# A planner that orders a fused attention and MLP kernel: new cost rules, weight checks tied to columns of h, and one leg less

## The chip, the cores and the metric

The kernel runs on one core of a Trainium2 chip. Its time is the device time of one execution in microseconds; the runs before are given by their median. The profile is of one further execution. Engines: PE (TensorE, matmuls), DVE (VectorE), ACT (ScalarE), POOL (GpSimd), SP (the queue that issues all DMAs).

## What is computed

Attention over 4 batches of 8 heads, 768 positions, head size 64, in which each query sees a window of 128 positions and the first 4 positions (sinks); then an MLP over the 3072 tokens with the square of a ReLU between its two products:

```python
scores = scale * np.matmul(q, k.transpose(0, 1, 3, 2))
keep = is_sink | in_window
scores = np.where(keep, scores, -1000000000.0)
a = np.exp(scores - max); a = a / (sum + 1e-09)
x = (a @ v) as 3072 x 512
h = np.maximum(x @ w_in, 0.0)          # 512 x 2048
out = (h * h @ w_out)                  # 2048 x 512
```

The weights arrive as 64-bit floats; the kernel reads them as pairs of 32-bit words.

## The kernel before

**Tiles.** The tokens are cut into 8 chunks of 384 (half a batch each). A chunk has 4 head pairs, so there are 32 pairs, numbered s = 0 to 31. The hidden layer is cut into 16 slices of 128; one slice of one chunk is called a column of h, and there are 8 x 16 = 128 of them.

**Attention of a pair** (`attention`, from L376): SP loads q (L402), two parts of k (L397) and v (L409). Scores are matmuls into a PSUM bank (L475 for the first 8 pairs, L481 after that, where DVE, POOL and ACT first split k and q into a high and a low part: L433, L438, L444, L449). DVE adds the mask and takes the minimum (L458), ACT exponentiates (L464), DVE makes reciprocals of the sums (L521, L522), POOL or ACT scale P (L529, L527). For the first 8 pairs P is turned by PE (L630); for the others by DVE in blocks (L660, L664), four DMAs to a DRAM tile `via` (L677) and one DMA back into `PT` (L690). The value product (L718, L722) gives 128 rows of x, which ACT and DVE split into xh (L734) and xl (L739). Two buffers of x exist (`xs`), chosen by the number of the chunk modulo 2.

**A column of h** (`products`, L754 on): the first product is 4 steps of 3 matmuls, 128x384 (L770), into one of two banks. ACT makes r, the ReLU (L783), and gh, its square (L787); DVE multiplies the bank by r (L792) and takes gh off it, giving the low part gl (L799). The second product is 3 steps, one to a block of 128 tokens, of 3 matmuls, 128x512 (L813), into three banks that collect over the columns of a leg. At a leg's end these are copied to `ob` (L854, DVE and ACT in turn) and stored.

**Legs.** The order in which chunks and slices are visited is a list of legs: chunk 0 slices 0 to 7, chunk 1 slices 0 to 7, chunk 0 slices 8 to 15, chunk 1 slices 8 to 15, then each later chunk whole. Where a leg ends at slice 8, its sums are stored to a DRAM tile `part` (L865) and reloaded later (L841) and added (L847).

**Weights** (`row_steps`): 32 rows of 512 KB, each loaded by SP (L283), put together from its words by three DVE operations (L295, L302, L309), copied to a high part by ACT (L315), and a low part is taken by DVE or POOL (L319).

**Checks** (`check_steps`): this way of splitting holds only for weights in a certain range, so each half row is loaded once more (64 loads of 256 KB, L331) into one of two buffers, and ACT runs two operations over it with a sum (L336, L343). At the end DVE and PE make a flag of all sums; if it is set, a second, general version runs (it does not here).

**The planner** (`Plan`) fixes each engine's order before anything runs. A step has one or more engines with a modelled cost, a rank, and cells that it reads and writes. `order` takes the steps one after the other: of the steps that may start first on an engine within 0.03 us, that with the lowest rank. A DMA is modelled with a landing time of its own, at most 8 in flight; a step whose kind is `"port"` does not start while POOL runs. A rank is the number of a column, or a number relative to it; ranks only decide between steps that are ready, so a step without inputs, as a check's load, is taken as soon as its buffer is free. Every engine then carries out its own list strictly in order and waits at each step for that step's inputs:

```python
add(
    ("SP", 0.4, 3.2), rank - 1,
    lambda: nc.sync.dma_start(out=half().rearrange("p w t -> p (w t)"), in_=words[n // 2, :, n % 2]),
    writes=[cell],
)
```

In this example 0.4 is the time on the queue, 3.2 the landing time, `rank - 1` when it is due, `cell` one of the two check buffers.

## Time and profile before

| | us |
|---|---|
| median of 3 runs | 722.74 (722.45 to 723.53) |
| the profiled execution | 726.08 |
| its span, first to last instruction | 724.3 |
| PE busy | 684.0 (94%) |
| DVE busy | 451.8 (62%) |
| ACT busy | 372.1 (51%) |
| POOL busy | 213.6 (29%) |
| mean granted clock of PE | 0.986 |

The profile counts an engine as busy while an instruction of its own runs. The granted clock is the share of full speed that PE's clock had. A row of a group gives line, engine, operation, tiles and count, then its busy time in us, the mean in ns of one, and the engine's idle time just before with what ended it. A row of waits gives who waited for whom: us in total, times, the longest. PEld is PE's loading of weights, which runs beside its matmuls. Line numbers are those of the kernel before; in the kernel after they are 8 to 10 higher from L295 on.

### The profile page before, as it was taken

Reading aid. Unit: us, or ns where it says so; the run is one execution under the profiler, and the core shown is the slowest. Engines: PE = TensorE matmul, PEld = TensorE weight load, DVE = VectorE, ACT = ScalarE, POOL = GpSimd, SP = SyncE. Lnnn points to the kernel's source line nnn. Section 1 sums busy time; section 2 is a strip of 40 time slices with the busy share of each in tenths; the row PEclk is TensorE's granted clock in tenths of the full one; section 3 lists DMA queues with packets and bytes.
Section 4 is the critical chain, followed back from the end, with each engine's and each line's share of the span. In section 5 each row is a group of like instructions: output and inputs, shape, how many; then the busy total and the mean of one; then the engine's idle time right before and its main releaser. Section 6 shows DMA issues by size and latency. Waiting matters only on the chain.

```text
span 724.3 us, 11379 instructions
## 1 busy us (share of the span) xinstructions
PE 684.0 (94%) x3722; PEld 581.9 (80%) x3722; DVE 451.8 (62%) x1207; ACT 372.1 (51%) x1058; POOL 213.6 (29%) x382
## 2 busy tenths in 40 slices
PE   6899999989989798989999999999999999999996
PEld 4566787877867687878988888889888888899885
DVE  6799999865656556656566776757556675232222
ACT  5778544577776667754444444444434443132221
POOL 3755525333223113331323333332232332000000
PEclk9999999999999899999999999999999999999999
DMA  8655564576787676654444543335444522100001
GB/s 248 212 184 173 197 228 151 154 233 210 254 258 230 215 246 194 201 155 120 126 130 142 149 133 109 113 92 144 125 130 144 155 92 85 48 16 28 1 1 48
DMA packets 59043, 106.36 MB, mean 147 GB/s; under 512 B 6304, under 2 KB 34720, under 8 KB 58976
## 3 DMA queue, kind: packets, MB, share of 16 engines
q1 hardware_dynamic: 58976, 105.56, 47.5%
q8 instruction: 31, 0.51, 0.3%
q14 instruction: 36, 0.29, 0.1%
HBM read 80.37 MB, written 25.17 MB: 146 GB/s over the span
## 4 chain that ended last, share of the span: by engine, by line
PE 56%; DMA 13%; DVE 13%; ACT 7%; POOL 5%; issue 4%; SPq 1%; DVEq 0%; ACTq 0%; POOLq 0%
PE bank L813 25%; PE bank L770 24%; DMA half<-in_moe_w_dram 9%; POOL P L529 4%; PE bank L481 3%; PE bank L718 3%; ACT sq L336 2%; DVE f L302 2%; DVE f L309 2%; ACT P L464 2%; DVE P L458 1%; DVE gl L799 1%; DMA part<-ob 1%; DMA out_dram<-ob 1%; DVE bank L792 1%
## 5 line engine op out<-in xcount | busy, mean ns | idle before, releaser
L770 PE MATMUL bank<-x,w 128*128 128x384 f32 x1536 | 352.0, 341 | 0.3 <-DVE x L739 0.3
L770 PEld LDWEIGHTS bank<-x,w 128*128 128x128 f32 x1536 | 271.6, 189 | 26.7 <-issue 1.4
L813 PE MATMUL bank<-w,gh 128*128 128x512 f32 x768 | 244.2, 399 | 14.4 <-ACT gh L787 9.5
L792 DVE TENSOR_TENSOR bank<-bank,r 128x384 f32<-128x384 f32 x128 | 71.6, 560 | 168.1 <-ACT r L783 167.9
L783 ACT ACTIVATE r<-bank 128x384 f32<-128x384 f32 x128 | 62.3, 487 | 189.1 <-PE bank L770 188.8
L813 PE MATMUL bank<-w,gl 128*128 128x512 f32 x384 | 155.1, 404 | 3.3 <-DVE gl L799 2.9
L813 PEld LDWEIGHTS bank<-w,gh 128*128 128x128 f32 x768 | 138.3, 189 | 23.3 <-ACT gh L787 13.0
L529 POOL TENSOR_SCALAR P<-P,small 128x264 f32<-128x264 f32 (+1 forms) x181 | 97.6, 555 | 162.1 <-DVE small L522 143.8
L438 POOL TENSOR_TENSOR KS<-kn,KS 128x408 fp32r<-128x408 f32 (+1 forms) x48 | 64.3, 1340 | 189.5 <-DVE KS L433 126.1
L464 ACT ACTIVATE P<-P,nbs 128x264 f32<-128x264 f32 (+1 forms) x192 | 94.7, 493 | 49.3 <-DVE nbs L458 48.0
L813 PEld LDWEIGHTS bank<-w,gl 128*128 128x128 f32 x384 | 72.4, 188 | 29.4 <-DVE gl L799 12.6
L799 DVE TENSOR_TENSOR gl<-bank,gh 128x384 fp32r<-128x384 f32 x128 | 70.0, 547 | 9.3 <-ACT gh L787 4.7
L787 ACT ACTIVATE gh<-r 128x384 fp32r<-128x384 f32 x128 | 67.0, 523 | 3.0
L660 DVE STREAM_TRANSPOSE T<-P 128x384 f32<-128x384 f32 x96 | 46.2, 496 | 25.2 <-POOL P L529 24.6
L458 DVE CUSTOM_DVE_ANT_0 P<-bank,maskA 128x264 f32<-128x264 f32 x128 | 52.7, 422 | 9.1 <-PE bank L481 7.1
L481 PE MATMUL bank<-KS,QS 128*128 128x264 f32 (+1 forms) x288 | 55.9, 283 | 1.5 <-DVE QS L449 0.8
L481 PEld LDWEIGHTS bank<-KS,QS 128*128 128x128 f32 x288 | 51.1, 190 | 6.2 <-DVE nbs L458 1.3
L336 ACT ACTIVATE sq<-half 128x256 bf16<-128x256 f32 x64 | 27.4, 427 | 35.5 <-DMA half<-in_moe_w_dram 34.9
L449 DVE TENSOR_TENSOR QS<-qn,QS 64x384 fp32r<-64x384 f32 x48 | 34.5, 718 | 8.3 <-ACT QS L444 7.0
L718 PE MATMUL bank<-PT,vn 128*64 128x256 f32 (+1 forms) x392 | 39.5, 341 | 0.0
L718 PEld LDWEIGHTS bank<-PT,vn 128*64 128x64 f32 x392 | 25.1, 136 | 14.7 <-issue 4.5
L464 ACT ACTIVATION_READ_ACCUMULATOR P<-P,nbs 128x1 f32 x192 | 36.0, 188 | 0.0
(89 smaller groups left out, 542.5 us busy)
## 6 DMA issues: line engine op xcount, KB each, us to landing
raw<-in_moe_w_dram SPq DMA_DIRECT2D x32, 512.0 KB, 3.6
half<-in_moe_w_dram SPq DMA_DIRECT2D x64, 256.0 KB, 3.7
via<-T SPq DMA_DIRECT2D x48, 192.0 KB, 3.4
PT<-via SPq DMA_DIRECT2D x12, 768.0 KB, 5.4
via<-T SPq DMA_DIRECT2D x48, 160.0 KB, 3.1
PT<-via SPq DMA_DIRECT2D x12, 640.0 KB, 5.3
kn<-in_k_dram SPq DMA_DIRECT2D x24, 272.0 KB, 4.1
qn<-in_q_dram SPq DMA_DIRECT2D x32, 192.0 KB, 2.7
```

Source lines behind the costliest of these rows:

```text
L438: lambda h=h: nc.gpsimd.tensor_tensor(KS(h)[:, 1, 0:nk], kn()[:, h, 0:nk], f32(KS(h)[:, 0, 0:nk]), op=ALU.subtract),
L458: nc.vector.tensor_tensor_reduce(Pt(h)[:, i, o : o + n], ps_[:, 0:n], mask[:, 0:n], -SCALE, BIG, ALU.add, ALU.min, nb)
L464: nc.scalar.activation(Pt(h)[:, i, o : o + n], Pt(h)[:, i, o : o + n], AF.Exp, bias=nb, scale=-1.0, accum_out=sm[:, h, i : i + 1],)
L481: nc.tensor.matmul(bank(key)[:, 0:n], QS(h)[:, cols], flat[:, a, c0 : c0 + n], start=(a == 0), stop=(a == 1),)
L529: {"POOL": nc.gpsimd, "DVE": nc.vector}[engine].tensor_scalar(a, a, rs[:, h, i : i + 1], 1.0, op0=ALU.mult, op1=ALU.mult)
L718: nc.tensor.matmul(xo[h * D : h * D + D, qs[0] * P : qs[0] * P + len(qs) * P], vn[:, kk, h, :], rhs(), start=(n == 0), stop=False, skip_gr ...
L770: nc.tensor.matmul(bank(key)[:, 0:TOK], wi[fc][:, i, cc * P : (cc + 1) * P], xt[:, cc, :], start=(cc == 0 and j == 0), stop=(cc == NCC - 1 ...
L783: lambda key=key, r=r: nc.scalar.activation(r(), bank(key)[:, 0:TOK], AF.Relu),
L787: ("ACT", 0.41), n - 9, lambda gh=gh, r=r: nc.scalar.activation(gh(), r(), AF.Square),
L792: lambda key=key, r=r: nc.vector.tensor_tensor(bank(key)[:, 0:TOK], bank(key)[:, 0:TOK], r(), op=ALU.mult),
L799: lambda key=key, gh=gh, gl=gl: nc.vector.tensor_tensor(gl(), bank(key)[:, 0:TOK], f32(gh()), op=ALU.subtract),
L813: nc.tensor.matmul(bank(okey), gt()[:, ts_], wo[f][:, i, :], start=(f == f0 and j == 0), stop=(f == f1 - 1 and j == 2),)
```

## The change

The planner gets new rules and numbers:

- DMA: each load carries its size in KB; a flow of 240 KB per us (`RATE`) delays its modelled landing, and 1 us (`LATE`) is added before anything that reads it may be planned.
- A PE step after a PE step may follow at once; a PE step after another engine's step follows 0.2 us (`AHEAD`) after that step's end instead of 0.06.
- The engines start at 0.5 to 5.5 us instead of all at 0.
- Six kinds of DVE operations with two inputs in SBUF (L302, L309, L319, L371, L449 and their like) are `"port"` now. The low part of a weight row costs 0.62 on DVE plus a handicap of 0.6 instead of 0.3.
- The reload of a part is due 4 columns ahead of its leg's end instead of 1.

Checks are planned from inside `products`: from the fifth leg on (chunk 3) one to a column; its load reads a cell `tick` that the first step of that column writes, so SP may issue it only once that matmul is done. Chunk 1 has one leg of 16 columns, set between the two legs of chunk 0, and the x buffers are handed out by a list `slot`. The diff's core:

```diff
-LOW_DVE = 0.3
+LOW_DVE = 0.6
+RATE = 240.0
+LATE = 1.0
+AHEAD = 0.2
+CHECK = 4
...
-        free = dict.fromkeys(("PE", "DVE", "ACT", "POOL", "SP"), 0.0)
+        free = dict(PE=0.0, DVE=5.5, ACT=1.5, POOL=5.0, SP=0.5)
...
             if e == "SP":
-                done = t + kind[0]
+                flow = max(flow, t + 1.3) + kind[1] / RATE
+                done = max(t + kind[0], flow + 0.7)
                 landed.append(done)
+                done += LATE
...
-                x["ready"] = max(x["ready"], done + self.HOP)
+                to_pe = x["at"][0][0] == "PE"
+                x["ready"] = max(x["ready"], free[e] if to_pe and e == "PE" else done + (AHEAD if to_pe else self.HOP))
...
+        slot = [0, 1] + [(c + 1) % 2 for c in range(2, NCHUNK)]
...
-                ("DVE", 0.6), rank,
+                ("DVE", 0.62, "port"), rank,
...
-                [("DVE", 0.6, "", LOW_DVE), ("POOL", 1.3)], rank, low, reads=[f_cell, ("w", n)], writes=[("wl", n)]
+                [("DVE", 0.62, "port", LOW_DVE), ("POOL", 1.3)], rank, low, reads=[f_cell, ("w", n)], writes=[("wl", n)]
...
-                ("SP", 0.4, 3.2), rank - 1,
+                ("SP", 0.4, 3.0, 262), rank + 0.5,
...
-                writes=[cell],
+                reads=[("tick", n_tick)], writes=[cell],
...
-                            writes=[(key, cc)], take=[("h", key)] if cc == 0 else [],
+                            writes=[(key, cc)] + [("tick", n)] * (cc == 0), take=[("h", key)] if cc == 0 else [],
...
+                    for x in checks.pop(fc, ()):
+                        check_steps(x, n, n)
...
-                    ("SP", 0.42, 2.8), n - 1, lambda: nc.sync.dma_start(out=ob(), in_=part[c, t]),
+                    ("SP", 0.42, 2.6, 262), n - 4, lambda: nc.sync.dma_start(out=ob(), in_=part[c, t]),
...
-        legs = [(0, 0, FH), (1, 0, FH), (0, FH, NFC), (1, FH, NFC)] + [(c, 0, NFC) for c in range(2, NCHUNK)]
+        legs = [(0, 0, FH), (1, 0, NFC), (0, FH, NFC)] + [(c, 0, NFC) for c in range(2, NCHUNK)]
...
-            products(c, f0, f1, starts[g])
-            nxt = {2: 2, 3: 3}.get(g, c + 2 if g > 3 else None)
+            own = {}
+            for fc in range(f0, f1) if g >= CHECK else ():
+                own[fc] = [checks.pop(0) for _ in range(min(1, len(checks)))]
+            products(c, f0, f1, starts[g], own)
+            nxt = g + 1
...
-            if g >= 3 and g < len(legs) - 1:
-                share = [checks.pop(0) for _ in range(min(16, len(checks)))]
-                for j, n in enumerate(share):
-                    check_steps(n, starts[g + 1] + j * (f1 - f0) / 16 if g > 3 else starts[g + 1] + j)
```

What this does to the lists is seen at three places. In the rows, `<-` stands between what is written and what is read; the first number in P, KS, QS, kn, qn and via is the pair, that in gh and gl is a column's number modulo 2, w_14 is the weight row of the first product's slice 7 and w_15 that of the second's.

PE in the kernel before, at slices 6 and 7 of chunk 1, where its first leg ended (w_16 is chunk 0's slice 8):

```order
L813 MATMUL bank7_74<-w_13_871,gh_0_555 128x512 x2
L813 MATMUL bank7_74<-w_13_871,gl_0_569 128x512
L770 MATMUL bank3_70<-x01_140,w_14_910 128x384 x2
L770 MATMUL bank3_70<-x11_141,w_14_910 128x384
L813 MATMUL bank6_73<-w_13_871,gh_0_555 128x512 x2
L813 MATMUL bank6_73<-w_13_871,gl_0_569 128x512
L770 MATMUL bank4_71<-x00_138,w_16_986 128x384 x2
L770 MATMUL bank4_71<-x10_139,w_16_986 128x384
L481 MATMUL bank0_67<-KS_9_1_1421,QS_9_1_1302 128x128 x2
L481 MATMUL bank1_68<-KS_9_1_1421,QS_9_1_1302 128x264 x2
```

The same place after (w_16 is chunk 1's own slice 8 here):

```order
L823 MATMUL bank5_72<-w_13_896,gl_0_590 128x512
L823 MATMUL bank7_74<-w_13_896,gh_0_578 128x512 x2
L823 MATMUL bank7_74<-w_13_896,gl_0_590 128x512
L823 MATMUL bank6_73<-w_13_896,gh_0_578 128x512 x2
L823 MATMUL bank6_73<-w_13_896,gl_0_590 128x512
L778 MATMUL bank4_71<-x01_140,w_16_996 128x384 x2
L778 MATMUL bank4_71<-x11_141,w_16_996 128x384
```

Before, the groups of the second product of slice 6 (w_13) stood between the steps of the first products of slices 7 and 8, and scores of pair 9 among the latter; one step, a score, one step, and then the second product of slice 7 follow. Now the three groups stand together, and after them all four steps of the next first product (the last two rows stand four times in a row there), then the second product of slice 7.

ACT in the kernel before, at the fourth column of chunk 2 (the names half are checks):

```order
L336 ACTIVATE sq_1558,wchk_122<-half_38_2555 128x256
L444 CAST QS_15_1_2606<-qn_15_2393 64x384
L464 ACTIVATE P_14_1_2550,small_135<-P_14_1_2550,nbs_125 128x264
L343 ACTIVATE sq_1558,wchk_122<-sq_1558,theta_123 128x256
L336 ACTIVATE sq_1558,wchk_122<-half_39_2590 128x256
L783 ACTIVATE r_1_567<-bank3_70 128x384
L343 ACTIVATE sq_1558,wchk_122<-sq_1558,theta_123 128x256
L787 ACTIVATE gh_1_581<-r_1_567 128x384
L336 ACTIVATE sq_1558,wchk_122<-half_40_2608 128x256
L343 ACTIVATE sq_1558,wchk_122<-sq_1558,theta_123 128x256
L734 CAST x01_140<-bank1_68 128x384
```

The same place after:

```order
L791 ACTIVATE r_1_586<-bank3_70 128x384
L452 CAST QS_15_1_2429<-qn_15_2288 64x384
L472 ACTIVATE P_14_1_2384,small_135<-P_14_1_2384,nbs_125 128x264
L795 ACTIVATE gh_0_578<-r_0_567 128x384
L472 ACTIVATE P_15_0_2438,small_135<-P_15_0_2438,nbs_125 128x264
L795 ACTIVATE gh_1_597<-r_1_586 128x384
L472 ACTIVATE P_15_0_2438,small_135<-P_15_0_2438,nbs_125 128x264 x2
L742 CAST x00_138<-bank0_67 128x384
L791 ACTIVATE r_0_567<-bank4_71 128x384
L795 ACTIVATE gh_0_578<-r_0_567 128x384
```

The checks between the columns' r and gh have gone, and here two columns' r stand ahead of the first of their gh. The first check now stands at chunk 3, and from there to chunk 6 a column has one.

SP in the kernel before, at the loads of pair 22, in chunk 4, where it had no checks left:

```order
L397 DMA kn_21_3660<-in_k_dram 64x2x544 x2
L677 DMA via_19_3691<-T_19_3613 32x4x320 x4
L690 DMA PT_134<-via_19_3691 128x4x320
L402 DMA qn_22_3829<-in_q_dram 128x384
L397 DMA kn_22_3835<-in_k_dram 64x2x544 x2
L409 DMA vn1_137<-in_v_dram 128x512
L677 DMA via_20_3870<-T_20_3785 32x4x384 x4
L690 DMA PT_134<-via_20_3870 128x1536
```

The same place after:

```order
L698 DMA PT_134<-via_19_3457 128x4x320
L339 DMA half_11_3579<-in_moe_w_dram 128x512
L339 DMA half_12_3620<-in_moe_w_dram 128x512
L405 DMA kn_22_3627<-in_k_dram 64x2x544
L410 DMA qn_22_3637<-in_q_dram 128x384
L405 DMA kn_22_3627<-in_k_dram 64x2x544
L417 DMA vn1_137<-in_v_dram 128x512
L685 DMA via_20_3676<-T_20_3564 32x4x384 x4
L339 DMA half_13_3693<-in_moe_w_dram 128x512
L339 DMA half_14_3727<-in_moe_w_dram 128x512
L698 DMA PT_134<-via_20_3676 128x1536
```

Two checks now stand ahead of the load of pair 22's k and two ahead of PT of pair 20.

More of the change, by code (lines that the diff above doesn't have):

```diff
@@ L92, in order @@
     def order(self):
-        free = dict.fromkeys(("PE", "DVE", "ACT", "POOL", "SP"), 0.0)
-        port, landed, mode = {"DVE": 0.0, "POOL": 0.0}, [], 0
+        free = dict(PE=0.0, DVE=5.5, ACT=1.5, POOL=5.0, SP=0.5)
+        port, landed, mode, flow = {"DVE": 0.0, "POOL": 0.0}, [], 0, 0.0
         open_ = [n for n, s in enumerate(self.steps) if s["waits"] == 0]
@@ L290, in row @@
                 return t
-            add(("SP", 0.5, 5.0), rank - 3, load, writes=[raw_cell])
+            add(("SP", 0.5, 3.6, 524), rank - 3, load, writes=[raw_cell])
             add(
@@ L307, in row_steps @@
             add(
-                ("DVE", 0.6), rank,
+                ("DVE", 0.62, "port"), rank,
                 lambda: nc.vector.scalar_tensor_tensor(
@@ L321, in row_steps, with check_steps @@
             add(
-                [("DVE", 0.6, "", LOW_DVE), ("POOL", 1.3)], rank, low, reads=[f_cell, ("w", n)], writes=[("wl", n)]
+                [("DVE", 0.62, "port", LOW_DVE), ("POOL", 1.3)], rank, low, reads=[f_cell, ("w", n)], writes=[("wl", n)]
             )
-        def check_steps(n, rank):
+        def check_steps(n, rank, n_tick):
             half = lambda: sb(f"f{n % 2}", [P, WR // 2, 2], I32, f"half_{n}")
@@ L358, in sinks @@
             add(
-                ("SP", 0.4, 3.0), rank - 4,
+                ("SP", 0.4, 2.6, 64), rank - 4,
                 lambda: nc.sync.dma_start(
@@ L369, in sinks @@
             add(
-                ("DVE", 0.6), rank,
+                ("DVE", 0.62, "port"), rank,
                 lambda: nc.vector.tensor_tensor(VS[lo], raw()[lo], f32(VS[lo]), op=ALU.subtract),
@@ L401, in attention @@
             add(
-                ("SP", 0.42, 3.3), rank(3.2), lambda: nc.sync.dma_start(out=qn(), in_=q[b, p, :, q0 : q0 + TOK]),
+                ("SP", 0.42, 2.7, 197), rank(3.2), lambda: nc.sync.dma_start(out=qn(), in_=q[b, p, :, q0 : q0 + TOK]),
                 writes=[q_cell],
@@ L405, in attention @@
             for a in range(2):
-                add(("SP", 0.57, 5.2 if plain else 4.2), rank(3.2), lambda a=a: load_k(a), writes=[(k_cell, a)])
+                add(("SP", 0.57, 4.0, 244 if not plain else 122), rank(3.2), lambda a=a: load_k(a), writes=[(k_cell, a)])
             add(
-                ("SP", 0.4, 3.0), rank(2.0),
+                ("SP", 0.4, 2.7, 49 * nk), rank(2.0),
                 lambda: nc.sync.dma_start(out=vn[:, 0:nk], in_=v[b, p, :, kb0 : kb0 + nk]), writes=[v_cell],
@@ L447, in attention @@
                     add(
-                        ("DVE", 0.585), r,
+                        ("DVE", 0.6, "port"), r,
                         lambda h=h, own=own, oth=oth: nc.vector.tensor_tensor(
@@ L683, in attention @@
                     add(
-                        ("SP", 0.42, 3.4), rank(0.8), lambda x=x: put(x),
+                        ("SP", 0.42, 3.2, 180), rank(0.8), lambda x=x: put(x),
                         reads=["T"] + [("T", h, which) for h in range(2) for which in range(3 - i0)],
@@ L688, in attention @@
                 add(
-                    ("SP", 0.42, 5.8), rank(0.5),
+                    ("SP", 0.42, 4.5, 720), rank(0.5),
                     lambda: nc.sync.dma_start(
@@ L731, in attention @@
             )
-            xh, xl = xs[c % 2]
+            xh, xl = xs[slot[c]]
             add(
                 ("ACT", 0.4), r - URGE, lambda: nc.scalar.copy(xh[:, p, :], bank(key_x)[:, 0:TOK]),
-                reads=[key_x], writes=[("xh", c % 2, p)],
+                reads=[key_x], writes=[("xh", slot[c], p)],
             )
@@ L739, in attention @@
                 lambda: nc.vector.tensor_tensor(xl[:, p, :], bank(key_x)[:, 0:TOK], f32(xh[:, p, :]), op=ALU.subtract),
-                reads=[key_x, ("xh", c % 2, p)], writes=[("xl", c % 2, p)], drop=[key_x],
+                reads=[key_x, ("xh", slot[c], p)], writes=[("xl", slot[c], p)], drop=[key_x],
             )
@@ L752, in sink_window_attention_moe, with products @@
         outs = [0]
-        def products(c, f0, f1, item):
-            xh, xl = xs[c % 2]
+        def products(c, f0, f1, item, checks):
+            xh, xl = xs[slot[c]]
             last = c == NCHUNK - 1
@@ L869, in evacuate @@
                 add(
-                    ("SP", 0.42, 2.4), n - 0.5, send,
+                    ("SP", 0.42, 2.2, 262), n - 0.5, send,
                     reads=[cell] if len(halves) == 1 else [(cell, x)],
@@ L894, in sink_window_attention_moe @@
             row_steps(n, row_rank(n))
-        checks = [n for n in range(2 * NROW)]
+        checks = list(range(2 * NROW))
         for g, (c, f0, f1) in enumerate(legs):
-            products(c, f0, f1, starts[g])
-            nxt = {2: 2, 3: 3}.get(g, c + 2 if g > 3 else None)
-            if nxt is not None and nxt < NCHUNK:
-                base, w = (starts[3], 2.0) if nxt == 2 else (starts[nxt + 2 - 1], 4.0)
+            own = {}
[3 more added lines that the diff above has]
+            nxt = g + 1
+            if 2 <= nxt < NCHUNK:
+                base, w = starts[nxt], (2.0 if nxt == 2 else 4.0)
                 if nxt % NHALF == 0:
```

2 lines of the change are left out of this document (1 added, 1 removed).

## Prediction

> **What bounds the kernel now.** I read the page's first rows, then the table of busy time by stretches, then TensorE's waits in the stretch that stands out, then the waits of ACT and of the DMA queue behind them. The first rows give the span and TensorE's share of it.
>
> ```profile
> span 724.3 us, 11379 instructions
> PE 684.0 (94%) x3722; PEld 581.9 (80%) x3722; DVE 451.8 (62%) x1207; ACT 372.1 (51%) x1058; POOL 213.6 (29%) x382
> ```
>
> TensorE (PE) is the bound, and no matmul goes away with this change, so what can be won is its idle time and its slow clock: 724.3 - 684.0 = 40.3 us idle. The table of stretches tells where these lie. Its columns are the stretch, its length, the busy time of PE, PE's weight loads, DVE, ACT and POOL (instructions in brackets), the granted clock, the DMA share and GB/s.
>
> ```profile
> 0.00:40.00 40.00, 30.06 (x174) 21.05 (x176) 30.16 (x113) 26.78 (x85) 21.03 (x50) 0.91 0.72 221
> 40.00:140.00 100.00, 94.92 (x529) 76.77 (x525) 97.88 (x223) 61.28 (x151) 45.92 (x59) 1.00 0.53 177
> 140.00:320.00 180.00, 161.79 (x858) 135.30 (x858) 105.66 (x299) 127.84 (x440) 52.79 (x101) 0.97 0.72 225
> 320.00:600.00 280.00, 279.81 (x1566) 246.01 (x1565) 178.58 (x485) 124.50 (x320) 90.10 (x162) 1.00 0.44 128
> 600.00:725.00 125.00, 117.47 (x603) 102.77 (x601) 39.51 (x93) 31.72 (x66) 3.74 (x10) 0.99 0.09 29
> ```
>
> PE idles 9.94 us at the start, 5.08 in 40 to 140 (where DVE is 98% busy), 18.21 in 140 to 320, 0.19 in 320 to 600, and 6.8 at the end, after its last matmul. The third stretch is the one to explain; it also has a granted clock of 0.97. PE's waits in that stretch, and the wait behind the second of them:
>
> ```profile
> PE bank L813 <- ACT gh L787: 9.5, 10, 1.8
> PE bank L813 <- DVE ob L847: 3.3, 1, 3.3
> PE bank L813 <- DVE ob L854: 1.6, 1, 1.6
> ...
> DVE ob L847 <- DMA ob<-part: 6.4, 2, 4.9
> ```
>
> Half of the idle time is the second product waiting for gh, which ACT makes. ACT has time enough (127.84 of 180 us), but it stands still in that stretch, and so does the DMA queue (SPq):
>
> ```profile
> ACT sq L336 <- DMA half<-in_moe_w_dram: 34.9, 24, 3.6
> SPq L331 <- ACT sq L336: 34.7, 41, 4.4
> ```
>
> The 64 weight checks use two buffers, so each load waits for an ACT read (34.7 us) and ACT then waits, in order, for the load (34.9 us). One instance from the timeline, ACT first, PE below:
>
> ```profile
> 235.21 0.43 ACT L336 ACTIVATE sq<-half 128x256 bf16<-128x256 f32 x1 [2.39 <-DMA half<-in_moe_w_dram]
> ...
> 236.27 0.47 ACT L783 ACTIVATE r<-bank 128x384 f32<-128x384 f32 x1
> 236.77 0.52 ACT L787 ACTIVATE gh<-r 128x384 fp32r<-128x384 f32 x1
> ...
> 237.35 0.73 PE L813 MATMUL bank<-w,gh 128*128 128x512 f32 x2 [0.50 <-ACT gh L787]
> ```
>
> ACT sits 2.39 us on a check's load, r and gh come behind it, and PE stops for 0.50 us. The idle time has a price after it too. The same columns around two of the waits, and under them from PE's timeline the matmuls that ended the longest ones:
>
> ```profile
> 170.00:175.00 5.00, 3.79 (x11) 3.11 (x12) 3.06 (x9) 4.13 (x15) 2.43 (x6) 0.68 0.82 213
> 240.00:245.00 5.00, 1.68 (x10) 1.36 (x9) 0.96 (x4) 3.68 (x13) 0.00 (x0) 0.85 0.91 315
> 245.00:250.00 5.00, 5.00 (x17) 4.71 (x18) 3.98 (x12) 2.35 (x8) 2.46 (x4) 0.50 0.46 172
> ```
>
> ```profile
> 146.34 0.73 PE L813 MATMUL bank<-w,gh 128*128 128x512 f32 x2 [1.62 <-DVE ob L854]
> ...
> 171.21 0.74 PE L813 MATMUL bank<-w,gh 128*128 128x512 f32 x2 [1.76 <-ACT gh L787]
> ...
> 244.78 1.22 PE L813 MATMUL bank<-w,gh 128*128 128x512 f32 x2 [3.32 <-DVE ob L847]
> ```
>
> Around the wait that ends at 171.21 the clock is 0.68, after the one that ends at 244.78 it is 0.50: 0.32 x 3.79 + 0.15 x 1.68 + 0.50 x 5.00 = 4.0 us lost.
>
> **The change part by part.** *Checks tied to columns.* All 64 leave the stretch 140 to 320 for the columns of chunks 3 to 6, one to a column, the load gated on the column's first matmul and planned to land 1 us later than modelled, so that ACT rarely waits. What each costs ACT, and what stands behind it:
>
> ```profile
> L336 ACT ACTIVATE sq<-half 128x256 bf16<-128x256 f32 x64 | 27.4, 427 | 35.5 <-DMA half<-in_moe_w_dram 34.9
> L336 ACT ACTIVATION_READ_ACCUMULATOR sq<-half 128x1 f32 x64 | 12.0, 188 | 0.0
> L343 ACT ACTIVATE sq<-sq,theta 128x256 bf16<-128x256 bf16 x64 | 32.2, 503 | 1.0
> L343 ACT ACTIVATION_READ_ACCUMULATOR sq<-sq,theta 128x1 f32 x64 | 12.0, 187 | 0.0
> L783 ACT ACTIVATE r<-bank 128x384 f32<-128x384 f32 x128 | 62.3, 487 | 189.1 <-PE bank L770 188.8
> L787 ACT ACTIVATE gh<-r 128x384 fp32r<-128x384 f32 x128 | 67.0, 523 | 3.0
> ```
>
> A check is 0.427 + 0.188 + 0.503 + 0.187 = 1.305 us of ACT, 64 of them 83.5 us. In 320 to 600 ACT goes from 124.50 to at most 208 of 280 us, 74%. Its cover there is the order of PE, which changes too. One column's first product and one group of the second, from PE's timeline late in the span:
>
> ```profile
> 693.21 2.27 PE L770 MATMUL bank<-x,w 128*128 128x384 f32 x12
> 695.33 0.63 PE L813 MATMUL bank<-w,gh 128*128 128x512 f32 x2
> ...
> 697.32 0.63 PE L813 MATMUL bank<-w,gh 128*128 128x512 f32 x2
> 697.79 0.39 PE L813 MATMUL bank<-w,gl 128*128 128x512 f32 x1
> 698.02 0.69 PE L770 MATMUL bank<-x,w 128*128 128x384 f32 x3
> ```
>
> Twelve matmuls of the first product take 695.33 - 693.21 = 2.12 us, three of the second 0.70. In the new order a column's h is followed by three such groups of the column before (2.1) and by all of the next column's first product (2.12), and only then by its own second product: 4.2 us. r and gh need 0.487 + 0.523 = 1.01, so 3.2 us of slack stand against a check's 1.305. In the old order one group and three of the four steps of a first product stood between, 0.70 + 3 x 2.12 / 4 = 2.3 us and some scores, so the wait for gh loses both its cause and its shortness of cover. Regrouping itself costs PE nothing: rows in both patterns run at the same pace.
>
> Of the 9.5 us of gh waits I keep 1.0: -8.5 (bounds -4.7, half stays, and -9.5). On the other side, if each of the 64 moved checks cost PE what the old ones did, 9.5 / 64 = 0.15 us, 9.6 us would come back; with the slack above I take +1.0 (bounds 0 and +9.6).
>
> *Second chunk in one leg.* One leg boundary goes, at 146 us, and with it three stores, three reloads and three additions; the ob wait of 1.6 us stands there: -1.6 (bounds 0, -1.6). The remaining reloads are due 4 columns ahead instead of 1, with no checks before them on SP, so the 3.3 us wait for a reload goes: -3.3 (bounds -1.6, -3.3). The other waits of that stretch, 18.21 - 9.5 - 3.3 - 1.6 = 3.8 us, stay: chunk 2's four pairs are now packed into some twelve columns, which is no easier on DVE.
>
> *The clock.* It fell after those waits; of 4.0 us I take back 3.3 (bounds -1.2, -4.0). [...]
>
> *The planner's other numbers.* They price three DVE operations and the low parts of weights as users of the shared port, move 8 of 21 low parts from DVE to POOL and 13 scalings of P from POOL to ACT, in the first 140 us.
>
> ```profile
> L319 DVE TENSOR_TENSOR w<-f,w 128x512 fp32r<-128x512 f32 x21 | 15.6, 748 | 0.4 <-ACT w L315 0.2
> L319 POOL TENSOR_TENSOR w<-f,w 128x512 fp32r<-128x512 f32 x11 | 16.2, 1470 | 30.2 <-ACT w L315 30.1
> ...
> PE bank L813 <- DVE gl L799: 1.8, 3, 0.7
> ```
>
> DVE gets rid of 8 x 0.748 = 6.0 us in a stretch where it is 98% busy; PE's part of that is small, since PE idles 5.08 us there, 1.8 of them for gl (last row, PE's waits in 40 to 140). With the longer cover of the new order I take -2.0 (bounds -5.0 and +5.8, the second from the first rival). At the start I take 0 (bounds -4 and +4, under half of 9.94 either way): loads, exponentials and transposes are reordered there, and which wait ends last no row tells. The end keeps its order: 0.
>
> **Sum:** -8.5 + 1.0 - 1.6 - 3.3 - 3.3 - 2.0 = -17.7 us. The profiled execution took 726.08 us and would take 708.4; the median of the runs before, 722.74, lies 3.34 below that execution, and the saving is taken off it: 705.0 us.
>
> **The rivals.** *The port takes it back.* Here is one low part on POOL and the DVE operation that met it:
>
> ```profile
> 50.14 1.65 DVE L309 SCALAR_TENSOR_TENSOR f<-raw,f 128x512 int32<-128x512 int32 x1
> ...
> 49.52 1.72 POOL L319 TENSOR_TENSOR w<-f,w 128x512 fp32r<-128x512 f32 x1 [3.01 <-ACT w L315]
> ```
>
> DVE's 1.65 us ends 0.55 after POOL's end at 51.24, so it did nothing before. Eight more low parts on POOL are 8 x 1.470 = 11.8 us of such standstill against 6.0 freed: +5.8 where I have -2.0, which gives 705.0 + 7.8 = 712.8 us. It decides if DVE meets most of them whole. For: DVE has hardly a gap there. Against: the new plan places both around the port. [...]
>
> *The queue stalls on gated checks, slower than before.* SP issues in order. In chunks 3 to 6 two checks now stand right ahead of PT and two ahead of kn, qn, vn and via of each head pair, each behind its column and its buffer. A mean wait of the row above is 34.7 / 41 = 0.85 us; two on the way of each of 16 pairs' PT are 1.7 us, 27 us in all, if the values come that late: 705.0 + 27 = 732 us. It cancels the gain from 17.7 / 16 = 1.1 us a pair. For: today's stretch shows exactly that coupling. Against: one check to a column of some 4.2 us is a third of the old crowd, and PE idles 0.19 us in 280 today, so pairs have lead.
>
> *Nothing comes of it.* The waits move from gh to chunk 2's packed pairs (DVE, POOL and the trip through via), and what is saved is lost there: 722.7 us. Against: DVE was 105.66 of 180 us busy in that stretch.
>
> **How the numbers follow.** The forecast has 0.71, the port 0.15, the queue 0.09, nothing 0.05. The two first are faster: 0.86; about 0.2%, 1.4 us, is what a measurement of this kernel can tell. The low end takes half of what the bounds add on the good side (1.0 + 1.0 + 0.7 + 3.0 + 4.0 = 9.7) and a little more, since the gated waits are only the idle time that shows: 697. The high end goes past the port's 712.8 by half of a bad start and of late checks (2.0 + 4.3 / 2): 717. Left out are the queue, nothing, and some 0.06 of the forecast's own tail.
>
> **What would show it.** Right: in the profile after, PE's waits for gh below 2 us, no wait for ob over 1 us, ACT's wait for check loads under 10 us and all checks after about 290 us, clock 0.99 or more in 140 to 320, PE idle there below 7 us, and at 320 to 600 below 2. Wrong: PE waiting for PT or KS in the later chunks (queue), DVE's L302 and L309 longer than today with PE waiting for gl or w before 140 us (port), PE idle of 15 us or more at 100 to 280 on scores (nothing), or a start that differs by over 4 us.

## The result, and the profile after

| | before | after |
|---|---|---|
| median, us | 723.13 (722.45 to 725.07, 4 runs) | 690.66 (688.96 to 691.48, 4 runs) |
| ratio | | 0.9544 (0.9517 to 0.957) |
| the profiled execution | 726.08 | 688.96 |
| its mean granted clock | 0.986 | 0.991 |

The kernel is faster, by 32.5 us between the medians; the forecast was a saving of some 18 us, to 705.0 us, with 697 as the low end. The profiled executions lie 37.1 us apart, one 3 us above its median, the other 1.7 below its own. What is read from the two traces below adds up to the larger figure.

The page's first rows after:

```profile
span 686.9 us, 11380 instructions
PE 667.4 (97%) x3722; PEld 581.1 (85%) x3722; DVE 459.1 (67%) x1194; ACT 375.0 (55%) x1073; POOL 215.2 (31%) x377
```

The table of stretches after, with the columns as before:

```profile
0.00:40.00 40.00, 29.48 (x174) 20.57 (x176) 28.40 (x113) 29.88 (x96) 17.83 (x45) 0.87 0.72 226
40.00:140.00 100.00, 97.64 (x550) 82.69 (x547) 96.65 (x195) 60.93 (x146) 44.46 (x52) 1.00 0.48 160
140.00:320.00 180.00, 179.30 (x1026) 157.75 (x1025) 128.09 (x363) 87.97 (x248) 68.15 (x127) 1.00 0.54 163
320.00:600.00 280.00, 280.00 (x1576) 247.62 (x1575) 180.90 (x469) 172.30 (x533) 84.78 (x154) 1.00 0.58 172
600.00:687.00 87.00, 80.95 (x405) 72.48 (x403) 25.10 (x56) 23.93 (x53) 0.00 (x0) 0.99 0.07 24
```

Two things are to be seen. PE's idle time fell by 20.8 us, from 40.3 to 686.9 - 667.4 = 19.5. And PE's busy time fell as well, from 684.0 to 667.4, by 16.6 us, although it still has the same 3722 matmuls. In 140 to 320 PE was busy 161.79 us with 858 matmuls before, 0.189 us each, and 179.30 with 1026 after, 0.175 each. At the pace after, 858 take 150.0 us: 11.8 us of the busy time there was no work (with the pace of before's own stretch 320 to 600, 279.81 / 1566 = 0.179, it is 8.5). With the idle time, 18.21 - 0.70 = 17.5 us, this one stretch gives 26 to 29 of the 37 us by this count, which mixes matmuls of several sizes; weighed by size it is 24.6 (end of the section on why the prediction was wrong). In 40 to 140 idle time fell by 2.7 us; at 0 to 40 and at the end each, by under 1 us either way.

The longest of PE's waits after, over the whole span:

```profile
PE bank L483 <- DMA kn<-in_k_dram: 5.1, 2, 4.6
PE bank L638 <- POOL P L537: 5.0, 4, 2.5
PE bank L823 <- ACT ob L864: 2.1, 1, 2.1
PE bank L778 <- DVE gl L807: 0.7, 1, 0.7
```

Of all, only the last of these lies after 140 us. No wait for gh is left at all. The waits of ACT and of the queue that belong to the checks, and when the queue issues these:

```profile
ACT sq L344 <- DMA half<-in_moe_w_dram: 1.0, 2, 0.6
...
SPq L339 <- ACT sq L344: 92.3, 34, 6.1
SPq L405 <- POOL KS L446: 89.0, 18, 12.3
...
L339 SPq DMA_DIRECT2D half<-in_moe_w_dram x64: 327/362/1202, 280.5 to 602.7; - x64
```

ACT hardly waits for a check's load. The queue waits for ACT more than before, 92.3 us against 34.7, now from 280.5 us on, and PE idles 0.00 us in 320 to 600: in this kernel the queue's waits cost PE nothing.

What PE's busy time hides is seen on its timeline. First come two places of the kernel before: the matmul ahead of the marked wait that ended at 146.34, and two rows in the stretch 245 to 250, at a granted clock of 0.50.

```profile
144.33 0.40 PE L813 MATMUL bank<-w,gl 128*128 128x512 f32 x1
...
247.63 1.16 PE L770 MATMUL bank<-x,w 128*128 128x384 f32 x3
248.59 0.64 PE L481 MATMUL bank<-KS,QS 128*128 128x264 f32 x2
```

And the same forms in the kernel after:

```profile
143.91 0.39 PE L823 MATMUL bank<-w,gl 128*128 128x512 f32 x1
144.14 0.40 PE L489 MATMUL bank<-KS,QS 128*128 128x264 f32 x2
144.37 1.75 PE L778 MATMUL bank<-x,w 128*128 128x384 f32 x9
145.96 0.33 PE L489 MATMUL bank<-KS,QS 128*128 128x128 f32 x2
```

A gl matmul of 128x512 lets the next one start 144.14 - 143.91 = 0.23 us later. Before, the next one started 146.34 - 144.33 = 2.01 us later: 1.78 us were lost and 1.62 are marked as idle, since the matmul's modelled end lies past the point at which the next could have started. And three matmuls of 128x384 take 248.59 - 247.63 = 0.96 us from start to start at that clock, 0.32 each, against (145.96 - 144.37) / 9 = 0.177 in the kernel after, where 1.00 was granted: all of it counts as busy.

### The profile page after: what moved, and what is told of

Its sections match the earlier page's. It is cut to its first block, busy times and chain, and to the rows that moved or that the text cites. A ratio compares the mean times of both kernels' runs of the same rounds, so it can differ in the third digit from the quotient of the medians.

```text
span 686.9 us, 11380 instructions
## 1 busy us (share of the span) xinstructions
PE 667.4 (97%) x3722; PEld 581.1 (85%) x3722; DVE 459.1 (67%) x1194; ACT 375.0 (55%) x1073; POOL 215.2 (31%) x377
## 4 chain that ended last, share of the span: by engine, by line
PE 90%; DVE 6%; ACT 1%; issue 1%; DMA 1%; SPq 0%; POOL 0%; DVEq 0%
PE bank L823 37%; PE bank L778 37%; PE bank L726 6%; PE bank L489 5%; PE bank L730 1%; DVE f L310 1%; PE bank L590 1%; PE bank L483 1%; DVE P L466 1%; PE bank L638 1%; DVE f L317 1%; DVE f L303 1%; DMA kn<-in_k_dram 1%; ACT w L323 0%; DVE w L327 0%
## 5 line engine op out<-in xcount | busy, mean ns | idle before, releaser
L778 PE MATMUL bank<-x,w 128*128 128x384 f32 x1536 | 303.1, 339 | 0.7 <-DVE gl L807 0.7
L778 PEld LDWEIGHTS bank<-x,w 128*128 128x128 f32 x1536 | 267.0, 188 | 9.5 <-issue 1.4
L823 PE MATMUL bank<-w,gl 128*128 128x512 f32 x384 | 151.4, 394 | 0.0
L537 POOL TENSOR_SCALAR P<-P,small 128x128 f32<-128x128 f32 (+1 forms) x168 | 88.5, 543 | 71.1 <-DVE small L530 48.9
L823 PEld LDWEIGHTS bank<-w,gl 128*128 128x128 f32 x384 | 72.1, 188 | 16.6
L807 DVE TENSOR_TENSOR gl<-bank,gh 128x384 fp32r<-128x384 f32 x128 | 70.9, 554 | 17.4 <-ACT gh L795 11.8
L742 ACT CAST x<-bank 128x384 fp32r<-128x384 f32 x32 | 15.3, 478 | 52.6 <-PE bank L730 52.4
L327 POOL TENSOR_TENSOR w<-f,w 128x512 fp32r<-128x512 f32 x19 | 27.1, 1430 | 51.4 <-ACT w L323 51.4
L529 DVE TENSOR_TENSOR small<-small,eps 128x3 f32<-128x3 f32 (+1 forms) x56 | 34.5, 616 | 3.3 <-ACT P L472 2.7
```

What stands on the lines that cost most here:

```text
L537: {"POOL": nc.gpsimd, "DVE": nc.vector}[engine].tensor_scalar(a, a, rs[:, h, i : i + 1], 1.0, op0=ALU.mult, op1=ALU.mult)
L778: nc.tensor.matmul(bank(key)[:, 0:TOK], wi[fc][:, i, cc * P : (cc + 1) * P], xt[:, cc, :], start=(cc == 0 and j == 0), stop=(cc == NCC - 1 ...
L807: lambda key=key, gh=gh, gl=gl: nc.vector.tensor_tensor(gl(), bank(key)[:, 0:TOK], f32(gh()), op=ALU.subtract),
L823: nc.tensor.matmul(bank(okey), gt()[:, ts_], wo[f][:, i, :], start=(f == f0 and j == 0), stop=(f == f1 - 1 and j == 2),)
```

## The experiments

Before them the theory was that the crowd of free-running checks is the cause: ACT and SP, each in order, stand for one another, and everything queued behind them comes late, not gh alone. Against it stood that the new order of PE does it by its longer cover, that the planner's new numbers (DMA, port, start times) place the work better, and that the single leg does. All runs are in this table, in the order of the text. "Saved" is against the kernel before on the same chip, whose medians were 723.26, 723.62, 724.4 and 722.9 for rows 1 to 4, 5 to 8, 9 to 12 and 13 to 16. The last column is ACT's wait for check loads in the profile.

| kernel | median, us | ratio | saved, us | ACT wait, us |
|---|---|---|---|---|
| before with checks tied to columns | 708.15 | 0.979 (0.9763 to 0.9817) | 15.1 | 31.2 |
| before with the PE rule | 718.24 | 0.9918 (0.9888 to 0.9948) | 5.0 | 32.9 |
| after, checks free as before | 700.6 | 0.9679 (0.9654 to 0.9705) | 22.7 | 3.0 |
| after, old PE rule | 694.38 | 0.9595 (0.9569 to 0.9621) | 28.9 | 1.5 |
| after, old DMA model | 695.23 | 0.9618 (0.9596 to 0.9641) | 28.4 | 20.1 |
| after, old port costs | 690.58 | 0.9552 (0.9531 to 0.9573) | 33.0 | 8.3 |
| after, old legs | 696.04 | 0.9638 (0.9605 to 0.9671) | 27.6 | 1.2 |
| after, old start times | 690.85 | 0.9549 (0.9525 to 0.9574) | 32.8 | 0.9 |
| before without checks | 701.19 | 0.9689 (0.9644 to 0.9734) | 23.2 | 0 |
| after without checks | 691.1 | 0.9556 (0.9512 to 0.9599) | 33.3 | 0 |
| checks, PE rule, legs | 714.99 | 0.9897 (0.9846 to 0.9948) | 9.4 | 67.9 |
| after, scaling of P moved to ACT | 690.13 | 0.9526 (0.9492 to 0.9559) | 34.3 | 3.7 |
| checks, PE rule, legs, DMA model | 690.06 | 0.9554 (0.9506 to 0.9602) | 32.8 | 8.9 |
| checks, PE rule, legs, reload's rank | 715.39 | 0.9898 (0.9867 to 0.9929) | 7.5 | 66.9 |
| after, no slack behind a landing | 690.64 | 0.9559 (0.951 to 0.9609) | 32.3 | 9.1 |
| checks, PE rule, legs, port costs | 694.77 | 0.9613 (0.9565 to 0.9661) | 28.1 | 23.0 |

**1. Before with the checks tied to columns.** One to a column from chunk 3 on, each load gated, and nothing else of the change.

```diff
-                ("SP", 0.4, 3.2), rank - 1,
+                ("SP", 0.4, 3.2), rank + 0.5,
...
-                writes=[cell],
+                reads=[("tick", n_tick)], writes=[cell],
...
+                    for x in checks.pop(fc, ()):
+                        check_steps(x, n, n)
```

> The kernel before with one part of the change alone: checks planned from products, one to a column from chunk 3 on, each load gated on its column's first matmul. Theory 1 (the crowd of checks, through ACT's and SP's in-order waits, was the main loss of 140 to 320 us): about 705 us, at least 15 below before, gh waits under 2 us, granted clock 0.98 or more. Theory 2 (the cover was the loss: products interleaved so that gh and gl were used too soon after the column's end): 712 to 718 us, since the short cover stays and other ACT work still comes between.

708.15 us: 15.1 of the 32.5 us by this one edit. PE's waits in this kernel, and ACT's for the loads:

```profile
PE bank L817 <- ACT gh L789: 2.3, 4, 1.1
PE bank L817 <- DVE ob L851: 1.7, 1, 1.7
...
ACT sq L338 <- DMA half<-in_moe_w_dram: 31.2, 22, 5.3
```

The waits for gh fall from 9.5 to 2.3 without the new order of PE. ACT still waits 31.2 us for loads, against 34.9 before, and in this plan the tied checks are not free. They run from 303.3 us on, and in 320 to 600 PE does 1537 matmuls, against 1565 in the kernel before without any checks (experiment 9), which takes 701.19 us: some 7 us of the checks' price are still there.

**2. Before with the new PE rule.** A PE step after a PE step may follow at once, one after another engine 0.2 us later.

```diff
-                x["ready"] = max(x["ready"], done + self.HOP)
+                to_pe = x["at"][0][0] == "PE"
+                x["ready"] = max(x["ready"], free[e] if to_pe and e == "PE" else done + (AHEAD if to_pe else self.HOP))
```

> The kernel before with one part alone: the planner lets a PE step follow a PE step at once and others 0.2 us after their end, so the products are grouped. Theory 1 (checks): 716 to 722 us, since ACT still stands on check loads for some 35 us and PE behind it. Theory 2 (cover): about 702 us or less, PE busy time near 668 instead of 684 us, gh waits under 4 us although ACT still waits some 30 us for check loads.

718.24 us, 5.0 saved. PE's waits, and the table of stretches at the longest of them:

```profile
PE bank L816 <- DVE ob L850: 7.8, 2, 5.9
...
PE bank L816 <- ACT gh L790: 0.5, 1, 0.5
```

```profile
240.00:245.00 5.00, 0.00 (x0) 0.00 (x0) 1.47 (x4) 4.00 (x15) 0.00 (x0) 0.91 0.90 324
245.00:250.00 5.00, 4.25 (x11) 3.58 (x12) 3.84 (x9) 2.22 (x7) 3.31 (x5) 0.50 0.50 176
```

The cover does what the prediction said: gh waits go, 0.5 us are left, with the checks still in their crowd. But most of the gain isn't there. The wait for a reload grows from 3.3 us to 5.9, and the granted clock is 0.50 behind it. How that wait hangs on the checks is read from the chain of work in the kernel before, from a check's load to PE (start, us, what):

```profile
230.51 4.62 DMA half<-in_moe_w_dram
...
235.21 0.53 ACT sq L336 x2
235.74 0.09 SPq L331
...
235.93 4.16 DMA out_dram<-ob
...
240.11 3.83 DMA ob<-part
...
244.04 0.70 DVE ob L847
...
244.78 1.22 PE bank L813 x2
```

SP can issue its next check only when ACT has read the buffer, which waited for the load ahead. The store of sums and the reload of others stand behind that check, 4.16 and 3.83 us one after the other, and PE stops 3.32 us.

**3. After with the checks as before.** All other parts of the change stay; the loads are free again and come from 141.6 us on.

```diff
-                reads=[("tick", n_tick)], writes=[cell],
+                writes=[cell],
...
+            if len(legs) - 7 <= g < len(legs) - 1:
+                share = [checks.pop(0) for _ in range(min(16, len(checks)))]
+                for j, n in enumerate(share):
+                    check_steps(n, starts[g + 1] + j)
```

> The kernel after with the checks put back to their old place (free to run as soon as a buffer is there, from chunk 2 on), the rest as after. Theory 1 (checks): 705 to 710 us, the gh waits back. Theory 2 (cover): 692 to 697 us, ACT's waits for check loads back at 25 us or more, PE's waits for gh still under 3 us.

700.6 us, 9.9 slower than after and between the two theories. The table of stretches where it is lost, and PE's timeline at its start:

```profile
215.00:220.00 5.00, 1.40 (x6) 1.05 (x6) 3.95 (x13) 1.69 (x7) 3.24 (x6) 0.81 0.96 336
220.00:225.00 5.00, 4.28 (x21) 2.57 (x19) 1.83 (x10) 2.89 (x12) 3.15 (x8) 0.50 0.97 276
225.00:230.00 5.00, 3.40 (x10) 2.52 (x10) 3.85 (x8) 3.50 (x8) 0.60 (x3) 0.50 0.80 266
230.00:235.00 5.00, 4.95 (x13) 4.37 (x14) 1.76 (x4) 0.83 (x4) 2.80 (x2) 0.50 0.56 199
235.00:240.00 5.00, 5.00 (x26) 4.25 (x27) 2.59 (x6) 1.02 (x2) 0.00 (x0) 0.98 0.33 87
```

```profile
217.84 0.59 PE L488 MATMUL bank<-KS,QS 128*128 128x264 f32 x2 [2.76 <-DVE nbs L465]
219.28 1.22 PE L488 MATMUL bank<-KS,QS 128*128 128x264 f32 x4 [0.85 <-DVE nbs L465]
```

Here PE waits for scores' minima, not for gh: free checks cost 9.9 us in this plan, by another chain than in the kernel before, where they cost 23.2 (experiment 9). ACT's wait for check loads is only 3.0 us in this kernel, which also speaks against taking that wait as the price. The DMA engines are 96 and 97% busy from 215 to 225 us, against 54% over 140 to 320 in the kernel after; whether it is their load or the order of the queue that makes the scores late was not told apart.

**4. After with the old PE rule.** Edit 2 undone.

> The kernel after with the old rule for when a PE step may follow a PE step or another engine's, the rest as after. Theory 1 (checks): 691 to 696 us. Theory 2 (cover): 703 us or more, PE busy time up by 8 us or more though no check runs before chunk 3.

694.38 us, 3.7 slower. The rule is worth less than its cover promised: with the checks out of the way, waits for gh come back as 1.2 us only. In 80 to 140, where DVE is nearly full, PE does 290 matmuls against 303 in the kernel after; but the kernels of experiments 8, 10 and 15, none of them slower than after, do 296, 295 and 285 there, so this count does not show where the 3.7 us went.

**5. After with the old DMA model.** `RATE`, `LATE` and the sizes go, the old landing times come back.

```diff
-                flow = max(flow, t + 1.3) + kind[1] / RATE
-                done = max(t + kind[0], flow + 0.7)
+                done = t + kind[0]
...
-                done += LATE
```

> The kernel after with the old model of DMAs (fixed landing times, no flow, no 1 us of slack), the rest as after. Of the 32.5 us that the change gave, checks gave 15.1 alone and the PE rule 5.0 alone, so 12.4 are with the other parts. If the DMA model carries them: 700 us or more, with waits for raw, kn or PT on the engines. If it is a refinement only: 690 to 694 us.

695.23 us, 4.6 slower and between the two expectations, though ACT waits 20.1 us for check loads.

**6. After with the old port costs.** The port marks that the change sets (five kinds of DVE operation) and `LOW_DVE = 0.6` go; 22 low parts are on DVE and 10 on POOL again, against 13 and 19 after.

> The kernel after with the old costs of DVE's two-input operations (no port) and the old handicap of DVE's low parts. If the relief of DVE before 140 us carries what is left: 696 us or more, with the loss in 40 to 140 us and the L302 and L309 operations longer in the mean. If the port takes back what the low parts on POOL free (the first rival of the prediction): 690 us or less.

690.58 us: no difference. Both things that the prediction tied to this part, DVE's relief and the rival that the port takes it back, are worth nothing in the finished kernel.

**7. After with the old legs.** Chunk 1 in two legs again, checks from the same chunk on.

> The kernel after with the old legs (chunk 1 in two, 6 stores and reloads instead of 3). By the prediction's term of one boundary: 692 to 693 us, the wait for an output buffer back near the end of column 16. If reloads matter more: 694 us or more.

696.04 us, 5.4 slower. PE's waits between 60 and 200 us in this kernel that the kernel after doesn't have:

```profile
PE bank L823 <- DVE ob L864: 1.5, 1, 1.5
PE bank L823 <- DVE ob L857: 1.4, 1, 1.4
PE bank L489 <- DVE QS L457: 1.2, 1, 1.2
```

Three waits, 4.1 us marked, account for most of the 5.4. In 80 to 140 PE does 287 matmuls here and 303 in the kernel after, but part of that is the clock, 0.97 here against 1.00 there. Both have a wait of 2.1 us for ACT's ob shortly before 100 us; in 100 to 105 the granted clock is 0.83 here and 1.00 in the kernel after. Experiment 10, no slower than after, has the same wait, a clock of 0.75 there and 295 matmuls.

**8. After with the old start times.** `dict.fromkeys(..., 0.0)` is back.

> The kernel after with all engines planned from time 0 instead of 0.5 to 5.5 us. By the prediction's term for the start (0, bounds -4 and +4): 687 to 695 us, the difference all before 40 us.

690.85 us: no difference, as the 0 in the sum said.

**9. Before without checks.** The list of checks is empty and their sums are zeroed.

> The kernel before with the weight checks left out (their sums are set to 0 once). This prices the crowd of checks by itself. Theory 1 (the crowd cost PE its waits of 140 to 320 us): about 703 us, 20 below before, and 5 below the run with the checks moved alone (708.15), which is what the moved checks cost where they are now in that kernel. If moving them cost nothing there: 707 to 709 us.

701.19 us: the checks cost the kernel before 23.2 us. In the prediction 9.5 us of waits for gh, 4.0 of clock and, with the reload's rank as a second cause, the wait of 3.3 us were tied to them, 16.8 at most. PE's waits without them:

```profile
PE bank L631 <- POOL P L530: 5.3, 6, 2.4
...
PE bank L814 <- DVE gl L800: 1.7, 4, 0.7
PE bank L814 <- DVE ob L848: 1.3, 1, 1.3
```

With the old order of PE and the old rank of the reload there is no wait for gh any more, and the waits for ob are down to 1.3 us. Experiment 1 lies 7 us above this kernel, where 5 were expected.

**10. After without checks.** The same edit in the kernel after.

> The kernel after with the weight checks left out in the same way. The prediction gave the moved checks +1.0 us (bounds 0 and 9.6): 689 to 690.7 us, ACT about 84 us less busy, PE the same. If each of them still costs PE 0.15 us: 681 us. If the gated loads stall the DMA queue (the second rival): 680 us or less.

691.1 against 690.66 us: 64 checks, 375.00 - 312.66 = 62.3 us of ACT's busy time and 16 MB of loads, cost nothing now. (That is 0.97 us of ACT for a check, not the prediction's 1.305: its four rows overlap, and the first two, 0.427 and 0.188 us, take 0.53 together in the chain of experiment 2.) So the change wins back the 23 us of the checks whole, and some 10 us (701.2 to 690.7) that have to do with other things.

**11. Checks, PE rule and legs, on the kernel before.** Edits 1 and 2 and the list of legs of the change; no DMA model, no port costs.

> The kernel before with three parts together: checks tied to columns, the PE rule, the second chunk in one leg; not the DMA model, the port costs, the start times and the earlier reload. Undoing parts of the change one at a time cost 10.0 (checks), 5.4 (leg), 4.6 (DMA model), 3.7 (PE rule), 0 and 0, together 23.7 of 32.5 us. If the rest is overlap among the three, they give all but the DMA model's share: 695 us. If the DMA model and the others carry more together: 700 us or more.

714.99 us: 9.4 saved, where the checks alone saved 15.1. ACT's wait for check loads is twice that of the kernel before (34.9 us) or of experiment 1 (31.2):

```profile
ACT sq L340 <- DMA half<-in_moe_w_dram: 67.9, 29, 5.8
```

Kernels 13, 14 and 16 look for what the rest of the change mends.

**12. After with 0.1 in place of 0.3 as ACT's handicap for scaling P.** It tries to shorten one of the two longest waits left, PE's for P (5.0 us, before 20 us).

> The kernel after with ACT's handicap for scaling P lowered from 0.3 to 0.1 us, so that ACT takes two of the first pair's six scalings again. In the profile after PE waits 5.0 us for POOL's scalings before 20 us, and the clock is 0.87 in the first 40 us. If that wait sets the start: 1 to 3 us less than after, 688 to 689.5 us (ratio 0.951 to 0.953). If the start is set by loads and DVE: 690 to 691 us.

690.13 us. The wait for P, with ACT's share, falls from 5.2 to 4.0 us, now mostly on ACT, and the time lies within the runs of after.

**13. Experiment 11 with the DMA model.**

> Checks tied to columns, PE rule, one leg and the DMA model together; not the port costs, the start times, the earlier reload. Theory A (a gated check's load, planned to land too early, stops ACT, and only the DMA model's later landing makes the checks free): 690 to 694 us, ACT waits under 5 us for check loads. Theory B (the loss of the three together is the late reload at the leg's end and chance in the order): 705 us or more.

690.06 us: these four parts give the whole gain, and the DMA model is worth 32.8 - 9.4 = 23.4 us in this company, 4.6 in that of experiment 5. The table of stretches of 11, ahead of the first check and with the checks:

```profile
140.00:280.00 140.00, 132.44 (x744) 114.58 (x743) 99.04 (x277) 63.45 (x176) 53.08 (x97) 0.99 0.51 151
280.00:600.00 320.00, 312.94 (x1735) 272.46 (x1735) 198.88 (x551) 186.93 (x581) 96.60 (x185) 1.00 0.53 167
```

And of 13:

```profile
140.00:280.00 140.00, 139.78 (x804) 122.46 (x803) 103.87 (x299) 67.22 (x185) 57.55 (x108) 1.00 0.56 163
280.00:600.00 320.00, 319.54 (x1793) 281.99 (x1792) 205.26 (x539) 194.99 (x598) 94.67 (x178) 1.00 0.54 171
```

In the first stretch 11 does 60 matmuls fewer, in the second 58: at 0.177 us some 10.5 us each. Before 140 it does 695 against 724 as well. The first check is issued at 310.0 us in 11, so more than half of the loss has nothing to do with checks. The longest wait of the first of these stretches in 11, with the queue's issue of the load, DVE's wait for it, and PE's:

```profile
192.03 1.26 SPq L401 DMA_DIRECT2D kn<-in_k_dram  x2
...
198.94 0.45 DVE L437 CAST KS<-kn 128x544 fp32r<-128x544 f32 x1 [1.33 <-DMA kn<-in_k_dram]
...
201.79 0.44 PE L586 MATMUL bank<-ident,PSK 128*128 128x128 f32 x2 [2.53 <-DVE nbs L462]
```

The load of k stands behind that of q, which waits for a buffer that DVE frees (its QS, 190.19 to 191.57). It lands late, DVE's list has what reads it ahead of the minima that PE needs, and PE stops. The QS is itself slow; its row, and that of POOL's operation beside it:

```profile
190.19 1.38 DVE L453 TENSOR_TENSOR QS<-qn,QS 64x384 fp32r<-64x384 f32 x1
...
189.79 1.37 POOL L442 TENSOR_TENSOR KS<-kn,KS 128x544 fp32r<-128x544 f32 x1 [0.38 <-DVE KS L437]
```

Others of its form take as little as 0.55 us in this stretch. The next QS at a busy POOL, at 199.77 and between the late KS and the minima, takes 1.50. The checks' loads may meet the same, a late load holding up whatever stands behind its reader; ACT's 67.9 us speak for it, but PE's marked waits from 280 to 600 us in 11 are 7.0 us, 4.7 of them for POOL, and no chain from a check's load to PE was followed there.

**14. Experiment 11 with the reload 4 columns ahead.**

> Checks tied to columns, PE rule, one leg and the earlier reload (4 columns ahead instead of 1); not the DMA model, port costs, start times. In the run without the earlier reload some 9 us of PE are lost between 180 and 220 us, with a 2.0 us wait for the reload. Theory A: 706 to 713 us, ACT still waits 20 us or more for check loads. Theory B: 700 us or less.

715.39 us, against 714.99: the rank of the reload does nothing in this company.

**15. After with `LATE = 0`.**

> The kernel after with the slack behind a modelled landing set from 1 us to 0, the flow kept. Theory A in its narrow form (the slack is what makes the checks free): 694 us or more, ACT waits 10 us or more for check loads. If the flow alone does it: 690 to 692 us, waits below 5 us.

690.64 us, though ACT waits 9.1 us for check loads: the slack of 1 us is not needed. The port costs are in this kernel too, so it does not show that the flow alone would do.

**16. Experiment 11 with the port costs.**

> Checks tied to columns, PE rule, one leg and the port costs with the low parts on POOL; not the DMA model, start times, earlier reload. Undoing the port costs alone in the kernel after changed nothing (690.58 us). If they matter without the DMA model: 708 us or less; if not: 712 to 716 us.

694.77 us: these numbers, worth nothing in experiment 6, give 28.1 - 9.4 = 18.7 us here. Thus either of two parts repairs the plan, this one all but 4.7 us of it, which is why taking one away from the finished kernel shows little. How they do it is open. From pair 10 on, k or one half of it stands ahead of q in the queue for all pairs but two; but experiment 13, which is faster, has q ahead of k for all pairs but two, as 11 has for all, so this order is not what repairs the plan there. The port costs are three things: a few hundredths of a us, a handicap that is 0.3 higher for low parts on DVE, and the rule that such a step is not planned beside POOL. QS falls under that rule: in 140 to 280 it takes 0.65 us in the mean here, against 0.84 in 11. In 13, without the rule, it takes 0.67. Which of the three does it was not tried by itself.

## Why the prediction was wrong

The side was right, the size was not: 690.66 us against 705.0.

- **The step that failed** is the premise under the sum: "what can be won is its idle time and its slow clock", 40.3 us idle. PE's busy time was taken as work. It fell by 16.6 us; the sum had 3.3 of that, as clock. The other 13.3 are most of what was missed: the profiled executions lie 37.1 us apart, the sum had 17.7. Idle time fell by 20.8 us, where the sum had 14.4. The rows to see it were in the prediction: 858 matmuls in 161.79 us in one stretch, 1566 in 279.81 in another. Between the two traces PE's busy time differs by 16.6 us for the same 3722 matmuls, PEld's by 0.8 (581.9 and 581.1).
- **Waits for gh, -8.5; the price of the checks.** The waits went, to nothing. But the crowd's price was read from the one wait behind ACT that stood out, with the clock and the reload's wait beside it, 16.8 us at most. It was 23.2 us (experiment 9): stalls hidden in busy time and other waits belonged to it.
- **The other waits, 3.8 us, "stay".** They did not: 0.70 us of idle time is left in 140 to 320. Tying the checks alone left 180 - 176.93 = 3.1 us there.
- **Late checks, +1.0 (up to +9.6).** They cost nothing in the finished kernel (experiment 10). The upper bound was not far off everywhere: in the plan of experiment 1 tied checks still cost some 7 us. ACT is 172.30 of 280 us busy in 320 to 600, not the 208 at most of the prediction, which took 1.305 us of ACT for a check where it is 0.97.
- **Reload, -3.3.** The wait went. Taking the checks away is enough for that (1.3 us are left in 9, with the old rank). The new rank did nothing where no crowd stands (14); with crowd and rank together, in 3, no wait for a reload is left either, so the rank's share is not settled.
- **One leg, -1.6.** Worth 5.4 in the finished kernel (7), where undoing it brings three waits, 4.1 us.
- **Clock, -3.3.** Granted 1.00 in 140 to 320, as forecast.
- **Early, -2.0; start and end, 0.** Idle time in 40 to 140 fell by 2.7 us. That term was the second that was too small: weighed by size, 8.8 us were won there (below). The reason given first, DVE's relief, is worth nothing in the finished kernel (6); which part won the 8.8 is not shown.
- **The cover of the new order.** As worked out: with the crowd in place 0.5 us of gh waits are left in 2, and none in 3. The crowd's price was not in that.
- **The rivals.** The port: no (6). The pair of rows behind it does show a slow DVE operation beside POOL, L309 with 1.65 us where the median of its 32 in the kernel before is 0.686; but undoing the port costs changed nothing. The queue on gated checks: it does wait, 92.3 and 89.0 us in the two rows, but PE idles 0.00 in 320 to 600; yet experiment 1 loses some 7 us by gated checks, and experiment 11, where ACT stands 67.9 us for their loads, some 10 us from 280 to 600 against 13: in a worse plan gated checks have a price. Nothing: no.
- **What was listed to show it.** gh below 2 us, ACT below 10, clock, idle time in both stretches: as listed. The checks begin at 280.5, not after 290, and one ob wait of 2.1 us is left, before 140 us.
- **The range.** 697 lies 8.0 us below 705.0, which is most of the 9.7 that the bounds add on the good side, while the text says half (4.9) and a little more; the high end adds a quarter of the 8.6 of late checks, where the text says half. The measured time lies below 705.0 - 9.7 = 695.3 too: the terms, not the choice within their bounds, were too small.

Where the profiled pair's 37.1 us lie can be told without the mixing of sizes: give each matmul the median time from start to start of its form where no idle time is marked, over the traces of all these kernels, and compare the two kernels at equal work done. Then before lies 0.5 us behind after at 40 us of after's time, 9.3 at 140, 33.9 at 320, 35.6 at 600 and 36.5 at the last matmul. So 8.8 us were won from 40 to 140, where the sum had 2.0 and only 2.7 show as idle time; 24.6 from 140 to 320, where it had 16.7; and 2.6 after that, where it had -1.0. The kernel before without checks (9) lies 6.5 us behind after at 140, 8.3 at 320 and 11.0 at the end: most of the 10 us that are not the checks' were won before 140.

Which part of the change owns which of these 10 us is not settled: undone one at a time, checks, legs, DMA model and PE rule cost 9.9 + 5.4 + 4.6 + 3.7 = 23.6 us, done in part they can even lose (11), so they are no terms of a sum.

## What to carry to other kernels

Before pricing what can be won on TensorE, divide its busy time by its matmuls, stretch by stretch and form by form: here a stretch with 0.189 us to a matmul, against 0.175 in the kernel after, held some 11.8 us of stalls and slow clock that no wait showed. A step that runs free and shares an engine's list with a chain of short lead can cost more than the wait that stands out behind it, here 23.2 us against 9.5; leave it out once and take the difference as its price in that plan. And the parts of a planner are not to be priced one at a time: each moves the lists in which the others work.

## What the runs showed of the hardware

The clock stayed halved for some 15 us in experiment 3: it was 0.81, 0.50, 0.50 and 0.50 in the four stretches of 5 us from 215 to 235, while PE idled 2.76 us, then 0.85 us and later up to 1.08 us at a time and was busy 1.40 us of the first 5, and it came back (0.98 in 235 to 240) after a stretch with 4.95 us of work in 5. After has no wait above 0.7 us past 140 us, and 1.00 from 140 to 600.

A wait of one length was not always followed by the same clock. PE's wait of 2.1 us for ACT's ob, which ends between 98 and 101 us, is followed in 100 to 105 by a granted clock of 1.00 in after and in experiment 3, and of 0.66, 0.75 and 0.83 in experiments 8, 10 and 7. The profiled execution of after, 1.7 us below its median, is one without that fall, so a difference of 1 or 2 us between two single traces can be this alone (an estimate: 5 us at 0.66 to 0.83 lack 1.7 to 0.9 us of full clock).

A wait of the DMA queue said little by itself: 198.3 us in all for one buffer, that of q, in experiment 11 and 165.1 in 13, which is 23.4 us faster.
